# Weights read as float64 words: the clamp first, the sign out of a parametric rectifier, roundings and most shifts on ScalarE

## The chip, the cores and the metric

One Trainium2 chip, one of its cores. The metric is the device time of one execution in microseconds (us), the median of several runs. In the profile PE is the matrix engine (PEld its weight loads), DVE the vector engine, ACT the scalar engine, POOL GpSimd, and SP issues the DMAs.

## What is computed

Eight batches pass through windowed attention (eight heads, half of them with a plain window, half with a dilated one), and then through a mixing block with four weight matrices, `w_theta`, `w_tok_r`, `w_tok_i` and `w_ch`:

```python
scores = np.where(masks[None], scale * np.matmul(q, k.transpose(0, 1, 3, 2)), -1e9)
attn = softmax(scores);  x = np.matmul(attn, v)        # to (8, 576, 512)
theta = x @ w_theta
y = einsum('ts,bsd->btd', w_tok_r, x * cos(theta)) + einsum('ts,bsd->btd', w_tok_i, x * sin(theta))
u = x + y
out = u + np.maximum(u @ w_ch, 0.0)
```

The matrices `w_theta`, `w_tok_r`, `w_tok_i` and `w_ch` come as float64, so the kernel gets each word as two 32-bit halves and has to make a float32 of them itself.

## The kernel before, in words

PE multiplies pairs of rounded parts: each operand is a high part in a rounded format (`fp32r`) and a low part, the difference, and a product takes three matmuls (high times high, high times low, low times high). The high part is a cast (L351, L354 for weights), the low part a subtraction on POOL (L356).

There are 18 pieces of weight. `unpack` (L302 on) makes float32 of one, and `split` (L347 on) makes the two parts:

- `st_wth`, 4 pieces of 512 columns (`theta_unpack` and, later, `theta_split`), used by the matmuls `th`;
- `st_wtk`, the token weights, 5 pieces for each half g of the output (four of 576 columns, one of 288). The pieces of g = 0 become `wtkh`, `wtkl`; those of g = 1 become `late_wt_a`, `late_wt_b`. They are used by the matmuls `y`;
- `st_wch`, the channel weights, 4 pieces of 512 columns, which become `late_wc`, used by the matmuls `c`.

A piece of float64 words is loaded by DMA into a staging tile. C is the view of its high halves, T that of its low halves. Before, a piece passes through these steps: C times 2^-112 on ACT (L323); T shifted right by 29 (L326 on ACT for the odd pieces of wth and of the first token half, L329 on DVE for all others); C clamped on DVE (L331); C shifted left by 3 and joined with T by an OR on DVE (L333). This loses the sign. Even pieces get it back by a Sign on ACT (L337) and a product on POOL (L339), odd ones by an AND and OR on DVE (L342). Then the cast: on DVE for wth and the first token half (L351), on ACT for the rest (L354).

The staging tiles are borrowed. The five token pieces of g = 1 lie in `u3`, `xh1`, `xh2`, `xh3`, `xh0`, and `st_wch` 0 to 3 in `xh2`, `xh3`, `xh2`, `xh3`. So `st_wch1` is loaded after the fourth late token piece is split, `st_wch3` after `st_wch1` is split, and only after `st_wch3` does `xh3` become free for the parts of the attention result of batch 1 (`xh`, L549 to L555), which its `th` matmuls read. Of the trigonometric part the reader needs that `K` (the phase, L692 to L694), the sine and cosine (`g`, L700 and L651), the products with `xn` (L656, L706, L713) and the rounding of the products (`zh` L594, `zl` L599) run on ACT, DVE, ACT, DVE, DVE and POOL, one after another, in two pairs of buffers.

The order on each engine is fixed in the program. For batch 0 and the parts of batches 1 and 2 that run beside it, a planner (class `Order`) sets it: each task names the engine and a cost before each operation, and a list of ranks (`RANK`) breaks ties. From batch 1 on, `phase` writes the order out by hand. Changing which operations a weight needs therefore reorders the beginning of the program.

```python
EARLY = ("u0", "u1", "u2", "u3", "xh0")
LATE = ("u3", "xh1", "xh2", "xh3", "xh0")
LATE2 = ("xh2", "xh3", "xh2", "xh3")
```

Of the kernel before, what the change touches and what calls it, by code (L numbers as in the profile page):

```python
# [12 lines left out]
AF = mybir.ActivationFunctionType  # L13
ALU = mybir.AluOpType
# [3 lines left out]
DM = H * D  # L18
# [30 lines left out]

W_MAX = 2.0 ** -96 * (2.0 - 2.0 ** -3)


class Order:
# [13 lines left out]
    def pin(self, ins):  # L69
        if self.live:  # L70
            self.tc.keep_in_program_order(ins)

    def signal(self, event):
        self.events[event] = self.now
# [49 lines left out]
def dve(n):  # L124
    return 67 + 1.04 * n


def dve2(n):
    return 67 + 0.52 * n


def act(n):
    return 95 + 0.83 * n


def pool(n):
    return 2.36 * n


def dma(n):  # L140
    return 128 * 4 * n / 360.0
# [3 lines left out]
def build(ctx, tc, qT, kT, vw, wth, wtk, wch, masks, ident, outT):  # L145
    nc = tc.nc
# [13 lines left out]
    pin, go, signal = od.pin, od.go, od.signal  # L160
# [20 lines left out]
    def take(tag, bufs, n=None):  # L181
        n = reserve(tag) if n is None else n
        if od.live:
            if n >= bufs:
                yield None, ("free", tag, n - bufs)
            if n:
                yield None, ("got", tag, n - 1)
            signal(("got", tag, n))
        return n

    def give(tag, n):
        if od.live:
            signal(("free", tag, n))
# [57 lines left out]
    def late(tag, words):  # L251
        if tag not in late_w:
            late_w[tag] = hp.tile([128, words], F32R, tag=tag, name=f"late_{tag}")
        return late_w[tag]
# [47 lines left out]
    def unpack(src, sz, name, stage, early, n, key):  # L302

        tag = None
        if stage is None:
            st = hp.tile([128, 2 * DM], F32R, tag=f"wc{n}", name=f"st_{name}{n}")
        else:
            tag = stage
            yield from take(tag[0], 1, tag[1])
            st = hp.tile([128, 2, S], F32R, tag=tag[0], name=f"st_{name}{n}").rearrange("p a b -> p (a b)")  # L310
        raw = st[:, :2 * sz].bitcast(U32)
        yield "DMA", dma(2 * sz)
        if len(src.shape) == 3:
            pin(nc.sync.dma_start(raw.rearrange("p (c b) -> p c b", c=src.shape[1]), src.bitcast(U32)))
        else:
            pin(nc.sync.dma_start(raw, src.bitcast(U32)))
        signal(("raw", name, n))
        yield None, ("raw", name, n)
        pair = raw.rearrange("p (a b) -> p a b", b=2)
        Ci, Ti = pair[:, :, 1], pair[:, :, 0]  # L320
        C, T = Ci.bitcast(F32), Ti.bitcast(F32)
        yield "ACT", act(sz)
        pin(nc.scalar.activation(C, C, AF.Copy, scale=2.0 ** -112))  # L323
        if early and n % 2:
            yield "ACT", act(sz)
            pin(nc.scalar.activation(Ti, Ti, AF.Copy, scale=2.0 ** -29, bias=-0.5))  # L326
        else:
            yield "DVE", dve2(sz)
            pin(nc.vector.tensor_scalar(Ti, Ti, 29, None, op0=ALU.logical_shift_right))  # L329
        yield "DVE", dve2(sz)  # L330
        pin(nc.vector.tensor_scalar(C, C, W_MAX, -W_MAX, op0=ALU.min, op1=ALU.max))  # L331
        yield "DVE", dve(sz)
        pin(nc.vector.scalar_tensor_tensor(out=Ti, in0=Ci, scalar=3, in1=Ti,  # L333
                                           op0=ALU.logical_shift_left, op1=ALU.bitwise_or))
        if n % 2 == 0:
            yield "ACT", act(sz)
            pin(nc.scalar.activation(C, C, AF.Sign))  # L337
            yield "POOL", pool(sz)
            pin(nc.gpsimd.tensor_tensor(T, T, C, op=ALU.mult))  # L339
        else:  # L340
            yield "DVE", dve(sz)
            pin(nc.vector.scalar_tensor_tensor(out=Ti, in0=Ci, scalar=0x80000000, in1=Ti,  # L342
                                               op0=ALU.bitwise_and, op1=ALU.bitwise_or))
        signal(key)
        return T, tag

    def split(T, sz, dst, early, key):  # L347
        hi, lo = dst
        if early:
            yield "DVE", dve2(sz)  # L350
            pin(nc.vector.tensor_copy(hi, T))  # L351
        else:
            yield "ACT", act(sz)
            pin(nc.scalar.copy(hi, T))  # L354
        yield "POOL", pool(sz)
        pin(nc.gpsimd.tensor_tensor(lo, T, hi.bitcast(F32), op=ALU.subtract))  # L356
        signal(key)

    wth32, wths, wtks, wchs = {}, {}, {}, {}

    def theta_unpack(c):
        T, _ = yield from unpack(wth[:, c], DM, "wth", None, True, c, ("wth32", c))
        wth32[c] = T

    def theta_split(c):
        for st in range(5):
            yield None, ("th0", st, c)
        wths[c] = tuple(cp.tile([128, DM], F32R, name=f"wth{h}{c}") for h in "hl")
        yield from split(wth32[c], DM, wths[c], True, ("wth", c))
        signal(("wc", c))  # L370

    def token_weights(g, n, stage):
        cs = slice(HS * g, HS * g + HS)
        c = 2 * n
        src, sz = (wtk[:, c:c + 2, cs], 2 * HS) if n < 4 else (wtk[:, c, cs], HS)
        T, tag = yield from unpack(src, sz, f"wtk{g}_", stage, g == 0, n, None)
        if g:
            for p in range(NP):
                yield None, ("pv", 0, p)
            t, o = (late("wt_a", 8 * HS), 4 * HS * n) if n < 2 else (late("wt_b", 10 * HS), 4 * HS * (n - 2))  # L380
            dst = tuple(t[:, o + i * sz:o + i * sz + sz] for i in range(2))
        else:
            dst = tuple(cp.tile([128, sz], F32R, name=f"wtk{h}{n}") for h in "hl")
        wtks[g, n] = dst
        yield from split(T, sz, dst, g == 0, ("wtk", g, n))
        give(*tag)

    def chan_weights(c, stage):
        T, tag = yield from unpack(wch[:, c], DM, "wch", stage, False, c, None)
        yield None, ("wc", c)  # L390
        t = late(f"wc{c}", 2 * DM)
        wchs[c] = tuple(t[:, DM * i:DM * i + DM] for i in range(2))
        yield from split(T, DM, wchs[c], False, ("wch", c))
        give(*tag)

    def mask_of(pr, j):
# [460 lines left out]
    for n in range(5):  # L857
        go(token_weights(0, n, EA[n]), RANK["token_early"] + n * .01)
    go(second_loads(), RANK["load"])
    for c in range(NC):  # L860
        go(theta_split(c), RANK["theta_split"] + c * .01)
    for n in range(5):
        go(token_weights(1, n, LA[n]), RANK["token_late"] + n * .01)
    for n in range(NC):
        go(chan_weights(n, LA2[n]), RANK["chan"] + n * .01)
# [80 lines left out]
```

## Time and profile before

| | |
|---|---|
| median of 3 runs | 617.66 us (617.5 to 617.88) |
| profiled execution: own time | 619.21 us |
| profiled execution: span | 617.4 us |
| busy: PE, PEld | 571.2 us (93%), 516.0 us (84%) |
| busy: DVE, ACT, POOL | 390.5 us (63%), 350.3 us (57%), 234.6 us (38%) |
| mean granted PE clock | 0.975 |

The span is what the instructions of the one profiled execution take; its own time has the launch around it. A busy share is a mean over the whole span. The first fifth of this span looks different from the rest, so stretches of it have to be read by themselves. In rows of a timeline the columns are start, duration, engine, line, operation, tile written and read, and in brackets the idle time before it and what ended that. Where rows are grouped, there are sums and means instead.

### The profile page before, as it was taken

The page shows a single profiled execution, that of the slowest core. Times are in us where ns is not written, and L with a number is a line of the kernel's source. Part 1 is how long each engine was busy: PE and PEld are TensorE (multiplying, and loading weights), DVE is VectorE, ACT ScalarE, POOL GpSimd, SP SyncE. Part 2 cuts the span into 40 slices and gives each one's busy share as a digit, 9 for nine tenths or more (in the row PEclk, how much of TensorE's full clock was granted, in tenths as well). Part 3 has the DMA queues.
Part 4 walks back from the last instruction along what each step waited for, and adds up shares of the span by engine and source line. Part 5 has one row for each costly group of instructions (what it writes and reads, how often), then busy time and mean ns, then how long its engine had stood idle before and what let it go on. Part 6 is the DMA issues. An engine that isn't in the chain of part 4 may idle for free.

```text
span 617.4 us, 14052 instructions
## 1 busy us (share of the span) xinstructions
PE 571.2 (93%) x5428; PEld 516.0 (84%) x5428; DVE 390.5 (63%) x1290; ACT 350.3 (57%) x951; POOL 234.6 (38%) x218
## 2 busy tenths in 40 slices
PE   4796687869999999999999999999999999999997
PEld 3543576858999889988999889998999899999997
DVE  4899998995566557656576556666576565535112
ACT  1885637737753594647843685638844685457110
POOL 2347665452432252242523153243523162414320
PEclk9998797969999999999999999999999999999999
DMA  8971425700354006420354017420454013000102
GB/s 327 397 282 38 137 98 167 252 12 19 118 175 155 2 21 221 152 76 1 136 176 157 2 39 234 137 59 2 161 156 151 1 49 107 19 0 30 49 1 78
DMA packets 26722, 67.82 MB, mean 110 GB/s; under 512 B 2848, under 2 KB 3104, under 8 KB 26656
## 3 DMA queue, kind: packets, MB, share of 16 engines
q1 hardware_dynamic: 26656, 66.92, 31.8%
q8 instruction: 43, 0.70, 0.5%
q14 instruction: 23, 0.19, 0.1%
HBM read 57.48 MB, written 9.44 MB: 108 GB/s over the span
## 4 chain that ended last, share of the span: by engine, by line
PE 45%; DVE 27%; ACT 20%; issue 3%; POOL 2%; DMA 2%; SPq 0%; ACTq 0%; DVEq 0%; POOLq 0%
PE y L750 23%; PE c L779 9%; DVE pt L486 8%; ACT P L464 6%; PE th L636 4%; PE s L438 4%; PE o L573 3%; DVE P L413 3%; ACT zh L597 2%; ACT K L651 2%; DVE K L656 2%; ACT g L700 2%; ACT K L649 2%; POOL P L470 2%; DVE st_wtk L333 1%
## 5 line engine op out<-in xcount | busy, mean ns | idle before, releaser
L733 POOL TENSOR_TENSOR u<-x,u 128x288 fp32r<-128x288 f32 x64 | 55.0, 860 | 179.4 <-ACT u L731 160.0
L779 PE MATMUL c<-u,late_wc 128*128 128x288 f32 x768 | 114.6, 300 | 6.2 <-ACT late_wc L354 2.6
L486 DVE STREAM_TRANSPOSE pt<-P 32x288 f32<-32x288 f32 x224 | 105.1, 469 | 21.2 <-POOL P L470 18.1
L779 PEld LDWEIGHTS c<-u,late_wc 128*128 128x128 f32 x768 | 107.9, 190 | 11.4 <-ACT late_wc L354 3.1
L731 ACT CAST u<-x 128x288 fp32r<-128x288 f32 x64 | 27.4, 429 | 133.2 <-DVE x L728 133.2
L464 ACT ACTIVATE P<-P,mx 128x64 f32<-128x64 f32 x252 | 84.1, 336 | 19.6 <-DVE mx L458 19.6
L750 PE MATMUL y<-wtkh,zh 128*128 128x288 f32 x288 | 90.4, 314 | 1.6 <-DVE zh L594 1.4
L750 PE MATMUL y<-wtkh,zl 128*128 128x288 f32 x288 | 86.3, 300 | 1.0 <-POOL zl L599 1.0
L750 PE MATMUL y<-wtkl,zh 128*128 128x288 f32 x288 | 86.1, 299 | 0.1
L599 POOL TENSOR_TENSOR zl<-g,zh 128x512 fp32r<-128x512 f32 x40 | 52.6, 1314 | 79.5 <-ACT zh L597 69.7
L636 PE MATMUL th<-wthh,xh 128*128 128x512 f32 x224 | 75.9, 400 | 0.0
L750 PE MATMUL y<-late_wt_b,zh 128*128 128x288 f32 x320 | 69.5, 300 | 3.5 <-ACT late_wt_b L354 2.1
L728 DVE TENSOR_TENSOR x<-y,x 128x288 f32<-128x288 f32 x64 | 28.7, 450 | 65.5 <-PE y L750 62.7
L750 PE MATMUL y<-late_wt_a,zh 128*128 128x288 f32 x256 | 57.9, 308 | 2.5 <-DVE x L728 2.5
L750 PEld LDWEIGHTS y<-wtkh,zh 128*128 128x128 f32 x288 | 55.3, 192 | 4.5 <-DVE zh L594 2.1
L470 POOL TENSOR_TENSOR P<-P,sm 128x576 f32<-128x576 f32 x32 | 38.4, 1200 | 49.1 <-DVE sm L468 24.1
L750 PEld LDWEIGHTS y<-wtkh,zl 128*128 128x128 f32 x288 | 55.1, 191 | 1.5 <-POOL zl L599 1.5
L599 POOL TENSOR_TENSOR zl<-K,zh 128x512 fp32r<-128x512 f32 x32 | 41.5, 1296 | 38.9 <-ACT zh L597 35.9
L750 PEld LDWEIGHTS y<-wtkl,zh 128*128 128x128 f32 x288 | 55.2, 192 | 0.9 <-issue 0.5
L750 PEld LDWEIGHTS y<-late_wt_b,zh 128*128 128x128 f32 x320 | 52.0, 190 | 4.7 <-ACT late_wt_b L354 2.3
L413 DVE CUSTOM_DVE_ANT_0 P<-s,msk 128x64 f32<-128x64 f32 x288 | 45.4, 219 | 14.2 <-PE s L438 13.9
L636 PEld LDWEIGHTS th<-wthh,xh 128*128 128x128 f32 x224 | 42.1, 188 | 8.0
(107 smaller groups left out, 1138.5 us busy)
## 6 DMA issues: line engine op xcount, KB each, us to landing
q<-in_qT_dram SPq DMA_DIRECT2D x32, 576.0 KB, 4.3
va<-in_vw_dram SPq DMA_DIRECT2D x30, 320.0 KB, 3.1
out_dram<-x SPq DMA_DIRECT2D x32, 288.0 KB, 2.1
k<-in_kT_dram SPq DMA_DIRECT2D x28, 304.0 KB, 4.7
vb<-in_vw_dram SPq DMA_DIRECT2D x29, 256.0 KB, 3.2
st_wtk<-in_wtk_dram SPq DMA_DIRECT2D x8, 576.0 KB, 8.3
st_wth<-in_wth_dram SPq DMA_DIRECT2D x4, 512.0 KB, 8.6
st_wch<-in_wch_dram SPq DMA_DIRECT2D x4, 512.0 KB, 3.9
```

Source lines behind the costliest of these rows:

```text
L413: pin(nc.vector.tensor_tensor_reduce(out=P[:, n], in0=ps[:, n - g0], in1=msk[:, mask_of(pr, n)], op0=ALU.add, op1=ALU.max, scale=1.0, scal ...
L438: pe(nc.tensor.matmul(ps[64 * e:64 * e + 64, n - g0], q[:, qb], k[:, QB * qb:QB * qb + BW], start=True, stop=True))
L464: table(nc.scalar.activation(P[:, n], P[:, n], AF.Exp, bias=mx[:, n:n + 1], scale=SCALE, accum_out=sm[:, n:n + 1]))
L470: pin(nc.gpsimd.tensor_tensor(P, P, sm.unsqueeze(2).to_broadcast([128, NJ, BW]), op=ALU.mult))
L486: pin(nc.vector.transpose(pmats[b, pr][hh][k0:k0 + QB, :, QB * e:QB * e + QB], P[p0:p0 + QB, :, QB * o:QB * o + QB]))
L599: pin(nc.gpsimd.tensor_tensor(lo, z, hi.bitcast(F32), op=ALU.subtract))
L636: pe(nc.tensor.matmul(pt, l, r, start=(n == 0), stop=(n == 3 * NC - 1)))
L728: pin(nc.vector.tensor_tensor(x[:, ts], ps, x[:, ts], op=ALU.add))
L731: pin(nc.scalar.copy(uh[b, d][:, ts], x[:, ts]))
L733: pin(nc.gpsimd.tensor_tensor(ul[b, d][:, ts], x[:, ts], uh[b, d][:, ts].bitcast(F32), op=ALU.subtract))
L750: pe(nc.tensor.matmul(ps, l[:, cs], r, start=(n == 0), stop=(n == 3 * NK - 1)))
L779: pe(nc.tensor.matmul(ps, l[:, cs], r[:, ts], start=(n == 0), stop=(n == 3 * NC - 1)))
```

## The change

In `unpack` the clamp is made first, on the raw high halves (its bound is larger by 2^112, so it cuts the same values). The scaling pass on ACT becomes a parametric rectifier, `Prelu` with alpha = -2^32: a positive C is scaled by 2^-112, a negative one becomes positive and larger by 2^32. That is a bit of the exponent which the shift left by 3 moves to the place of the sign, so the sign needs no steps of its own. The low halves are shifted on ACT except for the even pieces of wth and of the first token half. In `split` the cast is always on ACT. Lines behind these functions stand 12 lower in number than before (L486 is L474).

```diff
-W_MAX = 2.0 ** -96 * (2.0 - 2.0 ** -3)
+W_MAX = 2.0 ** 16 * (2.0 - 2.0 ** -3)
...
+        yield "DVE", dve2(sz)
+        pin(nc.vector.tensor_scalar(C, C, W_MAX, -W_MAX, op0=ALU.min, op1=ALU.max))
         yield "ACT", act(sz)
-        pin(nc.scalar.activation(C, C, AF.Copy, scale=2.0 ** -112))
-        if early and n % 2:
+        pin(nc.scalar.activation(C, C, AF.Prelu, scale=2.0 ** -112, alpha=-2.0 ** 32))
+        if early and n % 2 == 0:
+            yield "DVE", dve2(sz)
+            pin(nc.vector.tensor_scalar(Ti, Ti, 29, None, op0=ALU.logical_shift_right))
+        else:
             yield "ACT", act(sz)
             pin(nc.scalar.activation(Ti, Ti, AF.Copy, scale=2.0 ** -29, bias=-0.5))
-        else:
-            yield "DVE", dve2(sz)
-            pin(nc.vector.tensor_scalar(Ti, Ti, 29, None, op0=ALU.logical_shift_right))
-        yield "DVE", dve2(sz)
-        pin(nc.vector.tensor_scalar(C, C, W_MAX, -W_MAX, op0=ALU.min, op1=ALU.max))
         yield "DVE", dve(sz)
         pin(nc.vector.scalar_tensor_tensor(out=Ti, in0=Ci, scalar=3, in1=Ti,
                                            op0=ALU.logical_shift_left, op1=ALU.bitwise_or))
-        if n % 2 == 0:
-            yield "ACT", act(sz)
-            pin(nc.scalar.activation(C, C, AF.Sign))
-            yield "POOL", pool(sz)
-            pin(nc.gpsimd.tensor_tensor(T, T, C, op=ALU.mult))
-        else:
-            yield "DVE", dve(sz)
-            pin(nc.vector.scalar_tensor_tensor(out=Ti, in0=Ci, scalar=0x80000000, in1=Ti,
-                                               op0=ALU.bitwise_and, op1=ALU.bitwise_or))
...
-    def split(T, sz, dst, early, key):
+    def split(T, sz, dst, key):
         hi, lo = dst
-        if early:
-            yield "DVE", dve2(sz)
-            pin(nc.vector.tensor_copy(hi, T))
-        else:
-            yield "ACT", act(sz)
-            pin(nc.scalar.copy(hi, T))
+        yield "ACT", act(sz)
+        pin(nc.scalar.copy(hi, T))
```

The rest of the diff drops the argument `early` where `split` is called.

The change also reorders the instructions. First DVE, where the first token weights are made. `st_wtk0_0` to `st_wtk0_3` are the staging tiles of g = 0, `wtkh0` and `wtkh1` their high parts. Before:

```order
L331 TENSOR_SCALAR st_wtk0_1_189<-st_wtk0_1_189 128x576
L329 TENSOR_SCALAR st_wtk0_2_223<-st_wtk0_2_223 128x576
L333 SCALAR_TENSOR_TENSOR st_wtk0_1_189<-st_wtk0_1_189 128x576
L331 TENSOR_SCALAR st_wtk0_2_223<-st_wtk0_2_223 128x576
L342 SCALAR_TENSOR_TENSOR st_wtk0_1_189<-st_wtk0_1_189 128x576
L351 CAST wtkh0_529<-st_wtk0_0_145 128x576
L351 CAST wtkh1_541<-st_wtk0_1_189 128x576
L333 SCALAR_TENSOR_TENSOR st_wtk0_2_223<-st_wtk0_2_223 128x576
```

DVE at the same place now:

```order
L324 TENSOR_SCALAR st_wtk0_1_189<-st_wtk0_1_189 128x576
L334 SCALAR_TENSOR_TENSOR st_wtk0_0_145<-st_wtk0_0_145 128x576
L324 TENSOR_SCALAR st_wtk0_2_223<-st_wtk0_2_223 128x576
L334 SCALAR_TENSOR_TENSOR st_wtk0_1_189<-st_wtk0_1_189 128x576
L324 TENSOR_SCALAR st_wtk0_3_277<-st_wtk0_3_277 128x576
L329 TENSOR_SCALAR st_wtk0_2_223<-st_wtk0_2_223 128x576
L324 TENSOR_SCALAR st_wtk0_4_302<-st_wtk0_4_302 128x288
L334 SCALAR_TENSOR_TENSOR st_wtk0_2_223<-st_wtk0_2_223 128x576
```

The sign step L342 and the two casts are gone from DVE's queue; the clamps (now L324) stand ahead of the steps on ACT that they used to follow.

Second, DVE around the last channel weight, `st_wch3`. `pt` are the transposed probabilities of batch 2, `x0_2` the residual of batch 0. Before:

```order
L486 STREAM_TRANSPOSE pt0_103<-P2_0_1177 32x9x32 x2
L329 TENSOR_SCALAR st_wch3_1360<-st_wch3_1360 128x512
L728 TENSOR_TENSOR x0_2_407<-y0_2_1_1382,x0_2_407 128x288
L331 TENSOR_SCALAR st_wch3_1360<-st_wch3_1360 128x512
L486 STREAM_TRANSPOSE pt1_105<-P2_0_1177 32x9x32 x2
L333 SCALAR_TENSOR_TENSOR st_wch3_1360<-st_wch3_1360 128x512
L486 STREAM_TRANSPOSE pt1_105<-P2_0_1177 32x9x32 x2
L342 SCALAR_TENSOR_TENSOR st_wch3_1360<-st_wch3_1360 128x512
```

DVE at the same place now:

```order
L474 STREAM_TRANSPOSE pt0_103<-P2_0_1178 32x9x32 x2
L334 SCALAR_TENSOR_TENSOR st_wch3_1271<-st_wch3_1271 128x512
L474 STREAM_TRANSPOSE pt0_103<-P2_0_1178 32x9x32 x2
L716 TENSOR_TENSOR x0_2_417<-y0_2_1_1295,x0_2_417 128x288
L474 STREAM_TRANSPOSE pt1_105<-P2_0_1178 32x9x32 x2
```

Before, eight transposes of this group (one more pair stands ahead of the rows shown) and the residual `x0_2` come ahead of DVE's last step on `st_wch3`; now two transposes do.

Third, PE where the last token product of batch 0, `y0_3`, ends. `th1_4` is the first theta product of batch 1, `c0_0` and `c0_1` the first two channel products. Before:

```order
L750 MATMUL y0_3_1_1438<-late_wt_b_1069,zl0_8_624 128x288
L779 MATMUL c0_0_0_1487<-u0_0_842,late_wc0_1270 128x288 x3
L779 MATMUL c0_0_0_1487<-u0_1_896,late_wc1_1314 128x288 x3
L779 MATMUL c0_0_0_1487<-u0_2_970,late_wc2_1456 128x288 x3
L779 MATMUL c0_0_0_1487<-u0_3_1129,late_wc3_1492 128x288 x3
L779 MATMUL c0_1_0_1514<-u0_0_842,late_wc0_1270 128x288 x3
L779 MATMUL c0_1_0_1514<-u0_1_896,late_wc1_1314 128x288 x3
L779 MATMUL c0_1_0_1514<-u0_2_970,late_wc2_1456 128x288 x3
L779 MATMUL c0_1_0_1514<-u0_3_1129,late_wc3_1492 128x288 x3
L641 MATMUL th1_4_1526<-wthh0_670,xh1_0_1205 128x512
```

PE at the same place now:

```order
L738 MATMUL y0_3_1_1416<-late_wt_b_869,zl0_7_759 128x288
L629 MATMUL th1_4_1449<-wthh0_640,xh1_0_1141 128x512
L631 MATMUL th1_4_1449<-wthl0_641,xh1_0_1141 64x512
L628 MATMUL th1_4_1449<-wthl1_661,xh1_1_1139 64x512
L629 MATMUL th1_4_1449<-wthh1_660,xh1_1_1139 128x512
L628 MATMUL th1_4_1449<-wthl2_669,xh1_2_1266 64x512
L629 MATMUL th1_4_1449<-wthh2_668,xh1_2_1266 128x512
L628 MATMUL th1_4_1449<-wthl3_686,xh1_3_1418 64x512
L629 MATMUL th1_4_1449<-wthh3_685,xh1_3_1418 128x512
L738 MATMUL y0_3_1_1416<-late_wt_b_869,zh0_8_609 128x288 x2
L738 MATMUL y0_3_1_1416<-late_wt_b_869,zl0_8_610 128x288
```

The 8 matmuls of `th1_4` have moved ahead of the last 3 of `y0_3` and of the 24 of `c0_0` and `c0_1`, which now come behind the rows shown.

More of the change, by code (lines that the diff above doesn't have):

```diff
@@ L368, in theta_split @@
         wths[c] = tuple(cp.tile([128, DM], F32R, name=f"wth{h}{c}") for h in "hl")
-        yield from split(wth32[c], DM, wths[c], True, ("wth", c))
+        yield from split(wth32[c], DM, wths[c], ("wth", c))
         signal(("wc", c))
@@ L384, in token_weights @@
         wtks[g, n] = dst
-        yield from split(T, sz, dst, g == 0, ("wtk", g, n))
+        yield from split(T, sz, dst, ("wtk", g, n))
         give(*tag)
@@ L392, in chan_weights @@
         wchs[c] = tuple(t[:, DM * i:DM * i + DM] for i in range(2))
-        yield from split(T, DM, wchs[c], False, ("wch", c))
+        yield from split(T, DM, wchs[c], ("wch", c))
         give(*tag)
```

## The prediction

> **What bounds the kernel now.** I read the span by stretches first: theta of batch 0 (20 to 42.6 us), its sine and cosine up to the first exponentials of batch 1 (to 72.1), the token products up to the second set of token weights (to 96.9), and the rest up to `th1_4`, the first theta product of batch 1 (136.9). Columns: stretch and length, then busy us (and instructions) of PE, PEld, DVE, ACT, POOL, then the granted PE clock, the DMA share and GB/s.
>
> ```profile
> 20.00:42.60 22.60, 19.20 (x196) 10.12 (x195) 20.40 (x50) 19.47 (x47) 8.23 (x7) 1.00 1.01 380
> 42.60:72.10 29.50, 19.61 (x124) 12.16 (x122) 29.39 (x60) 17.05 (x27) 20.65 (x16) 0.83 0.18 57
> 72.10:96.90 24.80, 21.24 (x237) 18.96 (x237) 24.34 (x94) 14.51 (x67) 16.27 (x13) 0.93 0.43 147
> 96.90:136.90 40.00, 29.46 (x274) 25.93 (x274) 36.63 (x103) 23.83 (x78) 22.18 (x21) 0.82 0.43 141
> 136.90:617.40 480.50, 472.08 (x4446) 440.33 (x4444) 269.22 (x909) 270.21 (x723) 161.87 (x153) 1.00 0.26 86
> ```
>
> From 136.9 us on PE is busy 472.08 of 480.5 us, 98%: PE is the bound, and the change does not touch that work. Ahead of it DVE is busy 110.76 of 116.9 us (95%), while PE stands idle for 27.4 of them and gets a lower clock. So the first part runs at DVE's pace, and if it becomes shorter, all the rest starts earlier by as much. What ends the first part is seen on the timelines of PE and POOL:
>
> ```profile
> 132.29 0.85 PE L779 MATMUL c<-u,late_wc 128*128 128x288 f32 x2 [2.55 <-ACT late_wc L354]
> 133.66 3.49 PE L779 MATMUL c<-u,late_wc 128*128 128x288 f32 x13 [0.52 <-POOL late_wc L356]
> 136.95 0.63 PE L641 MATMUL th<-wthh,xh 128*128 128x512 f32 x1
> 132.31 1.29 POOL L356 TENSOR_TENSOR late_wc<-st_wch,late_wc 128x512 fp32r<-128x512 f32 x1 [3.03 <-ACT late_wc L354]
> 134.67 1.27 POOL L555 TENSOR_TENSOR xh<-x,xh 128x512 fp32r<-128x512 f32 x1
> ```
>
> PE waits for the last channel weight, whose low part POOL finishes at 133.60. The staging tile `xh3` then goes to `xh1_3`, finished at 135.94, one microsecond before `th1_4`. These two events are the gate.
>
> **What leaves DVE.** 26 instructions: 8 sign steps (L342), all 9 casts (L351), and the 9 late shifts (L329; the five early even ones stay). Groups of 20 to 137 us, the last but one column is the mean in ns:
>
> ```profile
> L342 DVE SCALAR_TENSOR_TENSOR st_wtk<-st_wtk 128x576 uint32<-128x576 uint32 x4 | 4.8, 1194 | 0.0
> L342 DVE SCALAR_TENSOR_TENSOR st_wch<-st_wch 128x512 uint32<-128x512 uint32 x2 | 1.4, 688 | 0.0
> L342 DVE SCALAR_TENSOR_TENSOR st_wth<-st_wth 128x512 uint32<-128x512 uint32 x2 | 1.4, 677 | 0.0
> L351 DVE CAST wthh<-st_wth 128x512 fp32r<-128x512 f32 x4 | 4.5, 1137 | 0.0
> L351 DVE CAST wtkh<-st_wtk 128x576 fp32r<-128x576 f32 x4 | 2.1, 536 | 0.0
> L351 DVE CAST wtkh<-st_wtk 128x288 fp32r<-128x288 f32 x1 | 1.0, 991 | 0.0
> ```
>
> Busy time: 7.6 and 7.6 us. For the shifts, DVE's busy time on L329 by the same stretches:
>
> ```profile
> 20.00:42.60 22.60, 1.77 (x4) 1.00 1.01 380
> 42.60:72.10 29.50, 3.78 (x3) 0.83 0.18 57
> 72.10:96.90 24.80, 2.33 (x3) 0.93 0.43 147
> 96.90:136.90 40.00, 1.80 (x4) 0.82 0.43 141
> ```
>
> The five that stay are the four of the first stretch and one of 1.38 us (the 288-column piece), so 9.68 - 1.77 - 1.38 = 6.5 us go. Together 21.7 us. But these instructions are longer than their work. Minimum, median and maximum in ns:
>
> ```profile
> L342 DVE SCALAR_TENSOR_TENSOR st_wtk<-st_wtk x4: 700/1046/1985, 39.3 to 97.8; 128x576 uint32<-128x576 uint32 x4
> L351 DVE CAST wthh<-st_wth x4: 411/1310/1517, 57.0 to 65.2; 128x512 fp32r<-128x512 f32 x4
> L351 DVE CAST wtkh<-st_wtk x5: 447/452/991, 40.0 to 70.6; 128x576 fp32r<-128x576 f32 x4, 128x288 fp32r<-128x288 f32 x1
> L329 DVE TENSOR_SCALAR st_wch<-st_wch x4: 380/428/564, 106.1 to 125.6; 128x512 uint32<-128x512 uint32 x4
> L329 DVE TENSOR_SCALAR st_wtk<-st_wtk x8: 300/692/1574, 33.1 to 95.1; 128x576 uint32<-128x576 uint32 x6, 128x288 uint32<-128x288 uint32 x2
> ```
>
> The long ones lie under POOL instructions, as here:
>
> ```profile
> 56.95 1.29 POOL L599 TENSOR_TENSOR zl<-g,zh 128x512 fp32r<-128x512 f32 x1 [1.02 <-DVE zh L594]
> 57.01 1.52 DVE L351 CAST wthh<-st_wth 128x512 fp32r<-128x512 f32 x1
> ```
>
> The cast starts 0.06 us after POOL's subtraction and ends 0.29 after it. Three more rows of DVE's timeline, and POOL's time on the sign products (L339), summed over the four stretches:
>
> ```profile
> 25.47 0.69 DVE L333 SCALAR_TENSOR_TENSOR st_wth<-st_wth 128x512 uint32<-128x512 uint32 x1
> 26.08 0.17 DVE L467 TENSOR_SCALAR sm<-sm 128x9 f32<-128x9 f32 x1
> 27.99 1.09 DVE L331 TENSOR_SCALAR st_wth<-st_wth 128x512 f32<-128x512 f32 x1 [1.50 <-ACT st_wth L323]
> sum 116.90, POOL 11.62; mean POOL 2.90
> ```
>
> Unhindered, the 26 would take 8 x 0.69 + 4 x 0.41 + 4 x 0.45 + 0.30 + 4 x 0.45 + 0.30 + 4 x 0.43 = 13.1 us, and neighbours overlap by 0.08 us (the second of these rows starts at 26.08, the first ends at 26.16), so DVE's queue is relieved of 13.1 - 26 x 0.08 = 11.0 us of work: **-11.0**.
>
> The other 8.6 us are holds behind POOL. A hold goes away with the instruction, unless the next DVE instruction runs into the same POOL instruction. POOL loses the ten sign products (11.62 of its 67.3 us in these stretches, last row above), so there is also less to run into. Bounds: 0 and 8.6; lacking a row for what the neighbours do I take half, **-4.2**.
>
> The Trainium skill (SBUF — State Buffer, "Who interferes with whom") has a rule for this: of a DVE operation that uses two ports and a GpSimd operation, the one that starts first keeps the shared ports for its whole instruction and the other is blocked, while ACT waits for nobody. The trace agrees (1.52 us beside 0.41). By that rule a cast that moves to ACT is never held, which would favour the full 8.6 us; it does not say whether the next DVE instruction inherits the hold.
>
> **What else moves.** The clamp now needs only the DMA: DVE's idle time of 1.50 us before L331 (row above) falls away, **-1.5**. Two transposes, a residual, and 18 matmuls `c` on the chain of waits:
>
> ```profile
> 123.21 0.94 DVE L486 STREAM_TRANSPOSE pt<-P 32x288 f32<-32x288 f32 x2
> 126.11 0.45 DVE L728 TENSOR_TENSOR x<-y,x 128x288 f32<-128x288 f32 x1
> 160.74 2.40 PE c L779 x18
> ```
>
> In DVE's queue six transposes (0.47 us each) and one residual (0.45) no longer stand ahead of the last step on `st_wch3`: **-3.2**; that they come later costs nothing there, since `pt` of batch 2 is read after `th1`. On PE, 27 matmuls (24 `c`, 3 `y0_3`) now come behind `th1_4`. Before, they were done when the gate opened. At 2.40 us for 18 they take 3.6 us, after the gate: **+3.6**.
>
> **What ACT gets.** Nine casts and nine shifts, less ten signs. Rows of casts, shifts and scaling passes on ACT, and the time of the signs (L337):
>
> ```profile
> L354 ACT CAST late_wc<-st_wch 128x512 fp32r<-128x512 f32 x4 | 2.6, 656 | 5.0 <-DVE st_wch L342 4.7 <-POOL st_wch L339 0.2
> L326 ACT ACTIVATE st_wtk<-st_wtk 128x576 uint32<-128x576 uint32 x2 | 1.6, 806 | 0.0
> L326 ACT ACTIVATE st_wth<-st_wth 128x512 uint32<-128x512 uint32 x2 | 1.4, 694 | 0.0
> L323 ACT ACTIVATE st_wtk<-st_wtk 128x576 f32<-128x576 f32 x8 | 5.9, 739 | 0.0
> sum 116.90, ACT 6.67; mean ACT 1.67
> ```
>
> 9 x 0.67 + 4 x 0.81 + 4 x 0.69 + 0.5 - 6.67 = 5.9 us more. ACT is idle for 42.0 of the 116.9 us, so I cost them at 0. That cover is thin in the first stretch, where ACT is busy 19.47 of 22.6, but there only 3 signs go and two casts come. No row shows `Prelu`; the nearest is the scaling pass that it replaces, 0.74 us at 576 columns. I take the same time; a tenth more in 18 passes would be 1.3 us, also in idle time. The program has as many ACT table loads as before.
>
> **The sum.** -11.0 - 4.2 - 1.5 - 3.2 + 3.6 = -16.3. The profiled span is 617.4 and its execution 619.21; the median of the runs, 617.66, stands within 0.3 of the span, so I subtract from that: 601.4 us.
>
> **Rivals.**
>
> ACT becomes the bound (0.20). A weight now passes DVE, ACT, ACT, DVE, ACT, POOL, and ACT's queue also carries sines and exponentials in order; a cast that waits for DVE's combine holds the sine behind it. If the added 5.9 us lie on the path: -10.4, 607.3 us. For it: ACT at 86% in the first stretch. Against: 58 to 60% in the three others. The Trainium skill (ScalarE: Activation LUTs, "Rules for kernel authors") speaks for this rival: it gives multiplications and the like to VectorE. The trace agrees for one cast alone, 0.41 against 0.66 us.
>
> All holds go (0.25): the full 8.6 us, -20.7, 597.0 us. For it: POOL's ten products are gone. If PE's clock also recovers in the last stretch (it loses 29.46 x 0.18 = 5.3 us there), half of that leads to 594.3.
>
> Slower (0.05). PE runs in order, so `th1_4` now blocks 27 matmuls that were ready. If `xh1_3` is not finished earlier, the time is 617.66 + 3.6 = 621.3. It decides if `xh1_3` ends later than 135.94 - 3.6 = 132.3. For it: the tile `xh3` still passes through two weights and two DMAs in turn. Against: every one of them comes out of DVE's queue.
>
> No change (0.02): gate and 3.6 us balance.
>
> **How the numbers follow.** My forecast has 0.48: 601.4. Measurement tells changes above 0.2% (1.2 us) from none. All cases but the last two are faster: 0.93, same 0.02, slower 0.05. The range of 594 to 611 takes in both ends of the holds, ACT's 5.9 us and some waits more; outside it lie the slower rival, no change, and a tenth for steps that I have mis-sized.
>
> **What would show it.** DVE's busy time falls by 15 to 22 us, ACT's rises by about 6, POOL's falls by 11 to 12. The first exponentials of batch 1 start near 65 us (72.1 now), the last channel weight's low part ends near 114 to 117 (133.60), and `th1_4` follows `xh1_3` at once. PE after that is as before. I am wrong if DVE stays at 95% up to `th1_4` with remaining instructions that have become longer, if waits for `st_` tiles appear before DVE's combine (L334) and cost more than 6 us, or if `xh1_3` comes later than 132.3 us.

## The result, and the profile after

The changed kernel takes 601.4 us (median of 4 runs, 600.39 to 603.07) beside 617.77 us for the kernel before on the same chip: ratio 0.9729, 95% interval 0.9697 to 0.9762. The profiled execution has a span of 599.8 us (617.4 before). The forecast was 601.4; the total came out, most of its terms did not, and most of what follows is about that.

First the gate, on the timelines of POOL and PE of the changed kernel:

```profile
113.52 1.29 POOL L344 TENSOR_TENSOR late_wc<-st_wch,late_wc 128x512 fp32r<-128x512 f32 x1 [3.21 <-ACT late_wc L342]
116.33 1.27 POOL L543 TENSOR_TENSOR xh<-x,xh 128x512 fp32r<-128x512 f32 x1
112.46 0.39 PE L629 MATMUL th<-wthh,xh 128*128 128x512 f32 x1
115.57 0.45 PE L628 MATMUL th<-wthl,xh 128*64 128x512 f32 x1 [1.57 <-ACT xh L537]
117.51 3.09 PE L767 MATMUL c<-u,late_wc 128*128 128x288 f32 x12
122.00 1.85 PE L767 MATMUL c<-u,late_wc 128*128 128x288 f32 x12 [1.40 <-DVE x L716]
```

The last channel weight is ready at 114.81 (133.60 before) and `xh1_3` at 117.60 (135.94): the gate comes 18.3 us earlier. From it to the end of the span it is 482.2 us, before 481.5, so 0.7 us are given back behind the gate: -18.3 + 0.7 = -17.6, the difference of the spans of the two profiled executions.

Next the stretch from 20 us to this gate, one row of the windows for each kernel (columns as before: stretch and length, busy us of PE, PEld, DVE, ACT, POOL, PE clock, DMA, GB/s). Before:

```profile
20.00:135.94 115.94, 88.54 (x823) 66.20 (x822) 109.83 (x302) 74.86 (x216) 67.33 (x55) 0.88 0.48 169
```

The changed kernel, and behind it what follows its gate:

```profile
20.00:117.60 97.60, 83.93 (x819) 62.44 (x818) 85.70 (x269) 77.63 (x219) 53.37 (x43) 0.91 0.57 201
117.60:599.80 482.20, 472.34 (x4458) 441.96 (x4456) 271.68 (x917) 272.17 (x732) 163.72 (x156) 1.00 0.25 86
```

DVE's busy time fell by 24.1 us, its idle time (length less busy) rose from 6.1 to 11.9 us, and -24.1 + 5.8 is the -18.3 of the gate. The 24.1 can't be set beside the 21.7 of the removed instructions as they are, for two reasons: neighbours overlap, so that durations add up to more than busy time, and DVE does 33 instructions fewer in the stretch, not 26. The other seven now stand behind the gate (four transposes, a residual and two small steps of a softmax; the changed kernel):

```profile
118.76 0.17 DVE L455 TENSOR_SCALAR sm<-sm 128x9 f32<-128x9 f32 x1 [1.60 <-ACT P L452]
118.97 0.21 DVE L456 RECIPROCAL sm<-sm 128x9 f32<-128x9 f32 x1
120.51 0.95 DVE L474 STREAM_TRANSPOSE pt<-P 32x288 f32<-32x288 f32 x2 [1.33 <-POOL P L458]
121.49 0.46 DVE L716 TENSOR_TENSOR x<-y,x 128x288 f32<-128x288 f32 x1
122.57 0.95 DVE L474 STREAM_TRANSPOSE pt<-P 32x288 f32<-32x288 f32 x2
```

If the 26 are taken out of the trace of before, the time that its other instructions cover is 18.5 us shorter; without these seven as well it is 21.1 us shorter. So of the 24.1 us 18.5 are the removed instructions, 2.6 are work put off until behind the gate, and 3.0 are left for the instructions that stay and became shorter on balance.

Most of the 5.8 are new waits for ACT (7.8 us in all, before 2.9), 0.9 are for POOL. DVE's largest waits in this stretch of the changed kernel (engine, line, what it waited for: us in total, times, longest):

```profile
DVE sm L455 <- ACT P L452: 3.0, 3, 1.4
DVE pt L474 <- POOL P L458: 1.6, 2, 1.4
DVE st_wtk L334 <- ACT st_wtk L332: 1.5, 2, 1.3
DVE K L682 <- ACT K L680: 1.5, 3, 0.7
DVE g L701 <- ACT g L688: 1.2, 1, 1.2
```

Before, DVE's largest wait in its stretch was the 1.50 ahead of the clamp.

Then the holds behind POOL (a hold is the time by which an instruction is longer than its work). Minimum, median and maximum in ns of the combine of the channel weights (L333, now L334) and of the cast `zh` of `K`. Before:

```profile
L333 DVE SCALAR_TENSOR_TENSOR st_wch<-st_wch x4: 683/1310/1682, 108.9 to 128.4; 128x512 uint32<-128x512 uint32 x4
L594 DVE CAST zh<-K x4: 406/412/538, 51.1 to 71.6; 128x512 fp32r<-128x512 f32 x4
```

The same two groups in the changed kernel, and the rectifier:

```profile
L334 DVE SCALAR_TENSOR_TENSOR st_wch<-st_wch x4: 693/726/1127, 86.9 to 112.1; 128x512 uint32<-128x512 uint32 x4
L582 DVE CAST zh<-K x4: 414/1509/1656, 47.8 to 67.4; 128x512 fp32r<-128x512 f32 x4
L326 ACT ACTIVATE st_wtk<-st_wtk x10: 472/732/777, 33.2 to 75.3; 128x576 f32<-128x576 f32 x8, 128x288 f32<-128x288 f32 x2
```

Instructions that the change leaves alone lost holds (the combine, median 1.31 to 0.73 us), and others got some (the cast `zh`, 0.41 to 1.51). One of these casts with the POOL instruction above it:

```profile
47.60 1.62 POOL L344 TENSOR_TENSOR wtkl<-st_wtk,wtkh 128x576 fp32r<-128x576 f32 x1
47.85 1.66 DVE L582 CAST zh<-K 128x512 fp32r<-128x512 f32 x1
```

`Prelu` takes 0.73 us at 576 columns, as the Copy that it replaces did.

### The profile page after: what moved, and what is told of

Read it like the earlier page. It is cut to its first block, busy times and chain, and to the rows that moved or that the text cites. A ratio compares the mean times of both kernels' runs of the same rounds, so it can differ in the third digit from the quotient of the medians.

```text
span 599.8 us, 14024 instructions
## 1 busy us (share of the span) xinstructions
PE 567.4 (95%) x5428; PEld 513.8 (86%) x5428; DVE 367.2 (61%) x1264; ACT 354.5 (59%) x959; POOL 222.5 (37%) x208
## 4 chain that ended last, share of the span: by engine, by line
PE 42%; DVE 25%; ACT 21%; DMA 5%; issue 3%; POOL 3%; SPq 0%; ACTq 0%; POOLq 0%; DVEq 0%
PE y L738 21%; DVE pt L474 11%; PE c L767 9%; ACT P L452 7%; PE o L561 4%; PE th L624 3%; DVE P L401 3%; PE s L426 3%; ACT zh L585 2%; ACT K L639 2%; DVE K L644 2%; ACT g L688 2%; ACT K L637 2%; POOL P L458 2%; PE th L606 2%
## 5 line engine op out<-in xcount | busy, mean ns | idle before, releaser
L474 DVE STREAM_TRANSPOSE pt<-P 32x288 f32<-32x288 f32 x224 | 105.1, 469 | 23.5 <-POOL P L458 20.4
L767 PE MATMUL c<-u,late_wc 128*128 128x288 f32 x768 | 112.9, 299 | 2.2 <-DVE x L716 1.4
L452 ACT ACTIVATE P<-P,mx 128x64 f32<-128x64 f32 x252 | 84.1, 336 | 17.6 <-DVE mx L446 17.4
L738 PE MATMUL y<-late_wt_b,zh 128*128 128x288 f32 x320 | 68.0, 296 | 0.0
L458 POOL TENSOR_TENSOR P<-P,sm 128x576 f32<-128x576 f32 x32 | 38.2, 1197 | 43.6 <-DVE sm L456 22.2
```

The lines of the kernel that those rows point to most:

```text
L452: table(nc.scalar.activation(P[:, n], P[:, n], AF.Exp, bias=mx[:, n:n + 1], scale=SCALE, accum_out=sm[:, n:n + 1]))
L458: pin(nc.gpsimd.tensor_tensor(P, P, sm.unsqueeze(2).to_broadcast([128, NJ, BW]), op=ALU.mult))
L474: pin(nc.vector.transpose(pmats[b, pr][hh][k0:k0 + QB, :, QB * e:QB * e + QB], P[p0:p0 + QB, :, QB * o:QB * o + QB]))
L738: pe(nc.tensor.matmul(ps, l[:, cs], r, start=(n == 0), stop=(n == 3 * NK - 1)))
L767: pe(nc.tensor.matmul(ps, l[:, cs], r[:, ts], start=(n == 0), stop=(n == 3 * NC - 1)))
```

## The experiments

All ratios are to the kernel before on the same chip. For comparison they are also turned into us of 617.8: the change itself is -16.7 in that measure (interval 14.7 to 18.7). In the runs named "order held" every engine executes its instructions in the changed kernel's order, and only the edit differs; that is possible because the planner sees only the cost lines, which stay. The gate is the end of `xh1_3` on POOL in the profiled execution. Line numbers of some runs stand higher than those of the change, by up to 8 in the lines shown.

| run | median us | ratio (95% interval) | us against before | gate us |
|---|---|---|---|---|
| the change | 601.4 | 0.9729 (0.9697 to 0.9762) | -16.7 | 117.60 |
| casts on DVE again | 605.08 | 0.9771 (0.9735 to 0.9808) | -14.1 | 120.34 |
| late shifts on DVE again | 604.88 | 0.9775 (0.9729 to 0.9821) | -13.9 | 120.19 |
| sign steps again | 617.97 | 0.9979 (0.9961 to 0.9996) | -1.3 | 134.03 |
| all three again | 624.78 | 1.0088 (1.0057 to 1.0119) | +5.4 | 140.19 |
| sign steps, DVE's alone | 604.65 | 0.9767 (0.9745 to 0.9789) | -14.4 | 121.24 |
| sign steps, product off the chain | 613.2 | 0.9918 (0.9895 to 0.9941) | -5.1 | 129.19 |
| before, sign and clamp alone | 605.75 | 0.9793 (0.9765 to 0.9822) | -12.8 | 123.44 |
| before, casts and shifts alone | 611.03 | 0.9885 (0.9852 to 0.9918) | -7.1 | not read |
| the change in the order of before | 612.1 | 0.989 (0.985 to 0.9931) | -6.8 | 127.56 |
| `th1_4` behind `c` | 602.74 | 0.9747 (0.9717 to 0.9776) | -15.6 | 118.00 |
| shorter staging chain | 602.83 | 0.975 (0.9727 to 0.9773) | -15.4 | 116.39 |
| `zh` casts on ACT | 603.42 | 0.9769 (0.9743 to 0.9796) | -14.3 | 119.55 |

**One part put back at a time, order held.** The theory was that DVE's queue sets the pace and each instruction costs its unhindered time and half its holds; the rivals were ACT's pace, and the order.

The nine casts:

```diff
-        pin(nc.scalar.copy(hi, T))
+        if key[:1] == ("wth",) or key[:2] == ("wtk", 0):
+            pin(nc.vector.tensor_copy(hi, T))
+        else:
+            pin(nc.scalar.copy(hi, T))
```

> The changed kernel (601.4 us) with its nine early weight casts (wth, first token half) on DVE again, each at the place in the program where ACT makes it now, all else in the same order. Theory of the sum: 9 instructions of 0.41 to 0.45 us unhindered, less 0.08 us overlap each, are 3.0 us of DVE's queue, and half of their 3.9 us of holds 1.9 more: +4.9, 606.3 us, with bounds of +3.0 (no hold comes back) and +6.9 (all). Rival, ACT is the pace: ACT is relieved of 6.2 us, so the time stays or falls, 599 to 601.5. Rival, the order does it and not the instructions: within 1 us of 601.4.

The nine shifts:

```diff
-            pin(nc.scalar.activation(Ti, Ti, AF.Copy, scale=2.0 ** -29, bias=-0.5))
+            if early:
+                pin(nc.scalar.activation(Ti, Ti, AF.Copy, scale=2.0 ** -29, bias=-0.5))
+            else:
+                pin(nc.vector.tensor_scalar(Ti, Ti, 29, None, op0=ALU.logical_shift_right))
```

> The changed kernel with the nine shifts of the late weights (second token half, channel weights) on DVE again, each at the place where ACT makes it now. Theory of the sum: 3.8 us unhindered less 0.7 overlap is +3.1, with half of the 2.7 us of holds +4.5: 605.9 us (bounds 604.5 and 607.2). Rival, ACT is the pace: 599 to 601.5. Rival, these shifts lie in time that DVE has over since the change (it is busy 85.7 of the 97.6 us from 20 us to the gate): under +1.5, 603.

The sign steps (values unchanged; `ones` is a column of ones, so here, unlike in the kernel before, the product does not wait for the Sign):

```diff
+        if n % 2:
+            pin(nc.vector.scalar_tensor_tensor(out=Ti, in0=Ci, scalar=0, in1=Ti,
+                                               op0=ALU.bitwise_and, op1=ALU.bitwise_or))
+        else:
+            pin(nc.scalar.activation(C, C, AF.Sign))
+            pin(nc.gpsimd.tensor_tensor(T, T, ones.to_broadcast([128, sz]), op=ALU.mult))
```

> The changed kernel with the work of the sign steps added again, without effect on the values: for odd pieces a DVE step of the form of L342, for even pieces a Sign on ACT and a product with ones on POOL, each behind DVE's combine, all else in the same order. Theory of the sum: 8 DVE steps of 0.69 less 0.08 us are +4.9, half of their 2.1 us of holds +1.0: 607.3 us; what ten POOL products of 1.16 us do to DVE's other instructions comes on top, up to the 3 to 4 us that the change took from holds of instructions that it left in place, 611. Rival, the order does it: under +1.5, 603.

All three:

> The three edits at once (casts, late shifts, sign steps back), the order still that of the changed kernel and the clamp still first. Theory of the sum: -11.0 and -4.2 are given back, 616.6 us, with bounds of 612.4 and 620.8; what is left to the kernel before (617.77) is order and clamp, -1.1. Rival, the order does most of it: below 609. If the three singles add up to much more or less than this one, their costs are not additive, which neither counted on.

Casts and shifts cost 2.6 and 2.8 us by the ratios, a little below the lower bounds of 3.0 and 3.1. Their intervals overlap that of the change, so the ratios alone don't show these costs; the gate comes 2.7 and 2.6 us later in the two profiles. A cost speaks against ACT's pace alone, by which the time would have stayed or fallen. The sign steps cost 15.4, far above the 9.6 (611 us) that were the most I allowed. The singles add up to 20.8, all three together cost 22.2: additive within the intervals. And all three together are 5.4 us slower than the kernel before, which has the same operations but for the place of the clamp and the product's wait for the Sign: the order of the change, with the sign steps set right behind the combine, does not suit the operations of before.

**Which part of the sign steps costs.** The DVE steps of the odd pieces alone (the first branch above):

> Half of the edit that cost 16.6 us when the sign steps came back: only the DVE steps of the odd pieces stand behind the combine again, without effect on the values; no Sign on ACT, no product on POOL; order of the changed kernel. If the steps on the even pieces (ACT, then POOL, ahead of the cast) made the excess over the sum: 8 x 0.61 us and half of 2.1 us of holds, +6.0, 607.4 us. If DVE's steps themselves were underpriced: 612 to 618.

2.3 us where 6.0 were expected, so 13.1 of the 15.4 belong to the even pieces, whose Sign on ACT and product on POOL the sum had priced only by the holds that they cause. Then the product moved off the weight's way: it does the same work, but writes where nobody reads (this run leaves the Sign out):

```diff
-            pin(nc.scalar.activation(C, C, AF.Sign))
-            pin(nc.gpsimd.tensor_tensor(T, T, ones.to_broadcast([128, sz]), op=ALU.mult))
+            pin(nc.gpsimd.tensor_tensor(C, T, ones.to_broadcast([128, sz]), op=ALU.mult))
```

> As the run in which all sign steps came back (618.0 us), but POOL's product writes into the dead high halves instead of the weight, and ACT's Sign is left out: POOL does the same ten products at the same places, still behind DVE's combine, and no cast, no theta product of batch 0 and no staging tile's cast waits for them. The DVE steps alone cost 3.2 us, so 13.3 us belong to the even pieces. If these come from the weights' longer way (combine, product, cast, and DVE waiting later): about 605 to 608. If they come from POOL's time itself (holds of DVE behind POOL, POOL's other work queued behind a product that waits for its combine): 613 to 618.

9.3 of the 13.1 us stay, though no weight waits for a product any more: they come from POOL's time. The other 3.8 are the longer way and the Sign, not told apart. Holds of DVE are little of it: up to the gate DVE is busy 92.43 us with all sign steps and 90.81 with DVE's alone. What is left is POOL's queue, and one place shows how it acts. The run with all sign steps, around `zl8` and `zl0`, POOL and then ACT:

```profile
56.51 1.44 POOL L595 TENSOR_TENSOR zl<-g,zh 128x512 fp32r<-128x512 f32 x1
59.16 0.67 POOL L343 TENSOR_TENSOR st_wtk<-st_wtk,ones 128x288 f32<-128x288 f32 x1 [1.21 <-DVE st_wtk L336]
59.78 1.27 POOL L595 TENSOR_TENSOR zl<-K,zh 128x512 fp32r<-128x512 f32 x1
61.09 0.60 ACT L688 ACTIVATE K<-th 128x512 int32<-128x512 f32 x1 [6.18 <-POOL zl L595]
```

The same place with DVE's sign steps alone:

```profile
50.21 1.44 POOL L590 TENSOR_TENSOR zl<-g,zh 128x512 fp32r<-128x512 f32 x1
51.62 1.33 POOL L590 TENSOR_TENSOR zl<-K,zh 128x512 fp32r<-128x512 f32 x1
52.98 0.60 ACT L683 ACTIVATE K<-th 128x512 int32<-128x512 f32 x1 [4.37 <-POOL zl L590]
```

Here `zl0` follows `zl8` at once. With the products it stands behind one that waits 1.21 us for DVE's combine and takes 0.67, and ACT, which needs the buffer of `K`, waits for `zl0`: 6.18 us instead of 4.37. So a product on an engine that is busy 38% of the span (56% up to the gate of this run) delays the next phase, by its place in an in-order queue. The place makes 1.8 us: ACT's row is 8.1 us later than in the other run, and 6.3 of them were there before it (56.51 against 50.21 for `zl8`). In the run with the product off the chain the wait is 6.23 us, so this place makes 1.9 of the 8.0 us by which its gate is later (129.19 against 121.24). The other places were not followed one by one; that they act in the same way is argued, not shown. These runs put each product right behind its combine; in the kernel before the planner placed them.

**One part alone, planner free.** The planner sets a new order in both runs: the kernel before with the clamp first and the sign out of the rectifier, and the kernel before with casts and shifts moved alone:

```diff
-        pin(nc.scalar.activation(C, C, AF.Copy, scale=2.0 ** -112))
+        pin(nc.vector.tensor_scalar(C, C, W_MAX, -W_MAX, op0=ALU.min, op1=ALU.max))
+        pin(nc.scalar.activation(C, C, AF.Prelu, scale=2.0 ** -112, alpha=-2.0 ** 32))
...
-        pin(nc.vector.tensor_scalar(C, C, W_MAX, -W_MAX, op0=ALU.min, op1=ALU.max))
...
-        if n % 2 == 0:
...
```

> The kernel before (617.8 us) with the clamp first and the sign out of the rectifier alone; casts and late shifts stay on DVE, and the planner sets the order anew. By the sum of the prediction: 4.9 us of DVE's queue, 1.0 of their holds, 1.5 for the clamp, -7.4, 610.4 us; if POOL's ten products held other DVE instructions too, to 606. If the sign is worth 16.6 us in any order: 600 to 603, and then the casts and shifts add nearly nothing to it.

> The kernel before with the nine early casts and the shifts moved as in the change, but the sign steps and the clamp as before; the planner sets the order anew. By the sum: 3.0 + 3.1 us of queue and half of their 6.6 us of holds, -9.4, 608.4 us. By what these two cost when they were put back one by one (3.7 and 3.5 us): 610.6. If the chain of the sign steps sets the pace, and DVE's queue is only second to it: above 614.

Sign and clamp alone, with the planner's new order, give 12.8 of the 16.7 us. The windows of that kernel:

```profile
20.00:123.44 103.44, 84.70 (x818) 63.65 (x813) 99.30 (x285) 69.81 (x206) 54.14 (x44) 0.93 0.54 189
```

DVE is still busy 96% of the time, and its busy time is down by 10.5 us. Counted as above, 6.4 of them are the eight steps of L342, holds and all, 3.3 are nine other instructions that now stand behind the gate (four transposes again), and only 0.8 are left for the instructions that stay. Products of POOL did hold some of those; here is one from the trace of before, and the clamp on DVE that starts 0.47 us after it and ends 0.32 after it:

```profile
37.53 1.55 POOL L339 TENSOR_TENSOR st_wtk<-st_wtk 128x576 f32<-128x576 f32 x1 [2.45 <-ACT st_wtk L337]
38.00 1.40 DVE L331 TENSOR_SCALAR st_wtk<-st_wtk 128x576 f32<-128x576 f32 x1
```

But other instructions became longer in turn (the four casts `zh` of `K`, 0.44 to 0.97 us on the mean). Idle time falls by another 2.0, and the gate comes 12.5 us earlier: while DVE is the bound, what it is relieved of does not come back as idle time. Casts and shifts give 7.1 us alone, but only 4.0 on top of the sign steps (0.9793 against 0.9729). The profiled execution of the kernel with casts and shifts alone took 617.49 us, 6.5 above its median, so nothing is read from its trace.

**The order.** All operations of the change, each where the operation that it replaces stood in the kernel before; only the clamp, which now has to come first, stands right ahead of the rectifier:

> All operations of the changed kernel, clamp first included, but every engine in the order of the kernel before (each operation stands where the one it replaces stood, th1_4 behind c0_0 and c0_1). By the sum the two terms for the order cancel (-3.2 and +3.6), and this kernel has -11.0, -4.2 and -1.5: 601.1 us. If each order suits only the operations it was planned for, as the run of 624.8 us (operations of before in the order of the change, 7.0 above the kernel before) makes likely: 605 to 609.

Only -6.8 us, 10 short of the change and less than either case had expected. Its windows, and DVE's largest waits up to its gate:

```profile
20.00:127.56 107.56, 86.86 (x811) 64.97 (x806) 85.22 (x277) 78.20 (x223) 54.73 (x45) 0.90 0.52 182
```

```profile
DVE sm L458 <- ACT P L455: 4.0, 4, 1.3
DVE K L685 <- ACT K L683: 3.3, 1, 3.3
DVE x L719 <- PE y L741: 3.1, 2, 2.9
DVE K L647 <- ACT K L642: 2.6, 3, 1.1
```

DVE is busy 85.2 us, as little as in the change (85.7), but idle 22.3 us instead of 11.9. The same relief is worth 8.4 us at the gate in the old order and 18.3 in the new one. What DVE gives up becomes waits, mostly for ACT, unless the planner fills them. The clamp at its new place does not leave DVE idle: it waits 0.2 us in all for the DMA of a staging tile.

**The 27 matmuls behind `th1_4`.**

```diff
     def thetas(b):
+        for e in range(2):
+            yield None, ("ch", 0, e, 0)
         for st in STS:
```

> The changed kernel with th1_4 behind c0_0 and c0_1 again, as in the kernel before; the rest of the planner's order follows from that. The prediction charged 3.6 us for the 27 matmuls that now come behind it, so by it this kernel gains up to 3.6: 597.8 us. By the trace of the change, six of the eight matmuls of th1_4 ran before the gate while PE had nothing else, and c0_0 and c0_1 stood behind waits of their own (1.40 us on a residual): a gain of at most 2, 599.4 to 601.4. Rival: th1_4 later means its sine chain later, and the transposes xn behind it wait: 602 to 604.

No gain: 602.74 us, where the two cases with a gain had 597.8 and up to 601.4; the interval overlaps that of the change. PE of this run:

```profile
114.67 1.85 PE L767 MATMUL c<-u,late_wc 128*128 128x288 f32 x12 [1.27 <-DVE x L716]
118.11 2.51 PE L767 MATMUL c<-u,late_wc 128*128 128x288 f32 x15 [1.59 <-DVE x L716]
120.46 0.39 PE L629 MATMUL th<-wthh,xh 128*128 128x512 f32 x1
```

Half of the `c` matmuls wait for a residual on DVE until 118.11, behind the gate, so only the other half could run ahead of it. From the gate to the end it takes 483.5 us, with the change 482.2.

**The staging tile.**

```diff
-LATE2 = ("xh2", "xh3", "xh2", "xh3")
+LATE2 = ("xh1", "xh2", "xh1", "xh2")
```

> The changed kernel with the channel weights staged in xh1, xh2, xh1, xh2 instead of xh2, xh3, xh2, xh3, so that the chain of three pieces through xh3 (fourth late token piece, st_wch1, st_wch3) ahead of xh1_3 becomes one of one piece. If this chain set the gate at 117.60 us (10.7 us from the DMA of st_wch3 to its low part): the gate comes 3 to 9 us earlier and the time falls to 593 to 599. If DVE's and ACT's queues set it, and the chain only fits into them: 600 to 602.5. Slower, if xh1_1 and xh1_2, which now wait for the channel weights, delay th1_4 more than xh3 gains: 603 to 606.

```profile
102.96 1.32 POOL L344 TENSOR_TENSOR late_wc<-st_wch,late_wc 128x512 fp32r<-128x512 f32 x1 [1.31 <-ACT late_wc L342]
115.10 1.29 POOL L543 TENSOR_TENSOR xh<-x,xh 128x512 fp32r<-128x512 f32 x1
```

The last channel weight is ready at 104.28 instead of 114.81, and `xh1_3` still ends at 116.39, 1.2 us earlier, with no gain in time. In the changed kernel the weights' chain only fits into the queues; it does not set the gate.

**One step further.** The casts `zh` of batch 0 on ACT too, order held:

```diff
         if b == 0:
             yield "DVE", dve2(DM)
-            pin(nc.vector.tensor_copy(hi, z))
+            pin(nc.scalar.copy(hi, z))
```

> The changed kernel with one more step in its own direction: the nine casts zh of batch 0 (L582) go from DVE to ACT, each at its place, the order held. They take DVE 8.4 us from 20 us to the gate (five of 0.42 us, four near 1.5, held behind POOL) and would take ACT about 9 x 0.66 = 5.9. If DVE still sets the pace: 595 to 599 us. If what DVE gives up now goes into waits for ACT (DVE's idle time rose from 6.1 to 11.9 us with the change): 600 to 603. If ACT has become the bound (80% busy up to the gate): 604 to 608. The cast stands between DVE's product and POOL's subtraction, in the chain that the next phase waits for on ACT.

```profile
20.00:119.55 99.55, 82.76 (x812) 61.76 (x812) 78.80 (x259) 81.68 (x226) 52.54 (x43) 0.93 0.56 197
```

DVE is relieved of 6.9 us more, and the gate comes 1.95 us later: its idle time is now 20.8 us. 603.42 us is just above the middle case, by which what DVE gives up goes into waits; moving these casts to ACT gains nothing in this order. By the Trainium skill (ScalarE: Activation LUTs, "Rules for kernel authors") `relu`, `max`, `min`, additions and multiplications belong on VectorE; it names neither casts nor shifts. Taken for such simple steps, the rule fits this last run, and it does not fit the casts and shifts of the change, which gained 4.0 us on ACT, with the order that the planner made for them.

## Why the prediction was right, and where it was not

DVE's queue did set the pace, so the way and the rough size were right; that the total of -16.3 us came out so closely was luck, since errors of several us cancelled. The terms, and what the two profiled executions (spans 617.4 and 599.8) show for each:

| term | forecast, us | shown, us |
|---|---|---|
| the 26 instructions that leave DVE, with holds | -11.0 - 4.2 | -18.5 |
| work of DVE that now stands behind the gate | -3.2 | -2.6 |
| instructions of DVE that stay | 0 | -3.0 |
| DVE's idle time up to the gate (clamp, ACT) | -1.5 + 0 | +5.8 |
| PE behind the gate | +3.6 | +0.7 |
| sum | -16.3 | -17.6 |

- **The bound.** Right: with DVE at 95% of the stretch, the kernel with the sign steps gone gained at the gate what DVE lost, and idle time did not grow. PE behind the gate stayed as it was, 0.7 us longer.
- **Queue relief and half of the holds, -11.0 - 4.2.** Too small by 3.3, and 3.0 more came from instructions that stay. So holds went as the rival "all holds go" had it, and somewhat beyond. The step that failed is the half, taken for lack of a row (half of 8.6 is 4.3, too; the sum took 4.2). A hold can pass on to another instruction, as I had reckoned: the four casts `zh` of `K` are 3.3 us longer (1.8 to 5.1 us in all). More was lost than passed on. How much of that is due to POOL's ten products is not settled: with the order held they lengthen DVE's busy time by 1.6 us (90.81 to 92.43), and with the sign steps gone and the order new only 0.8 us went from what stays. By the Trainium skill (SBUF — State Buffer, "Who interferes with whom") the blocked one of the two waits for the other's whole instruction; the pair of product and clamp above agrees, with the clamp ending 0.32 us after the product.
- **ACT at 0.** This is the error the other way. DVE's idle time rose by 5.8 us, 4.9 of it in waits for ACT, though ACT had 20% of the stretch idle after the change. Free time on an engine is no cover when the work is a step in a chain, or stands in the queue ahead of one: DVE's combine waited 1.5 us for shifts on ACT (`st_wtk`, L334 for L332), and DVE waited longer than before for exponentials and phases that ACT also makes (3.0 us on `sm`, 1.5 on `K`). ACT as a bound was a rival at 0.20, and it took part of the gain, while DVE's relief gave more than forecast.
- **The sign steps.** Priced at 4.9 and about 1 us of holds, with 1.5 for the clamp: -7.4, measured -12.8. At the gate it was 6.4 for the steps and 2.0 of idle time, 8.4 together; the rest is mainly the 3.3 of work that the new order put behind the gate. The product's place in POOL's queue, ahead of the subtractions `zl`, was not in the sum at all; the runs with the order held show that ten products cost there (9.3 us, where products stand right behind their combine). How much of the 12.8 this makes in the kernel before's own order is not measured.
- **Casts and shifts.** 3.0 + 3.1 of queue and 3.3 of holds, -9.4 together; measured -4.0 on top of the sign steps, and -7.1 alone.
- **Clamp first, -1.5.** DVE's wait of 1.50 for ACT before the clamp is gone from the list of waits. It was not run alone.
- **Six transposes and a residual, -3.2, and 27 matmuls, +3.6.** Two terms for the order with a sum of +0.4. The first was near: 2.6 us of DVE's work went behind the gate, four transposes, the residual and two small steps. But the order as a whole was worth about -10: the change in the order of before has only -6.8. The prediction looked at two places of the order and left out that the planner fills DVE's waits everywhere. The +3.6 is 0.7 by the time behind the gate, and putting `th1_4` back gained nothing.
- **What would show it.** The first exponentials of batch 1 start at 65.75 (forecast near 65), the last low part ends at 114.81 (114 to 117), POOL's busy time falls by 12.1 (11 to 12), and waits for `st_` tiles before L334 are under 2 us. DVE's fell by 23.3 over the whole span (15 to 22), ACT's rose by 4.2 (about 6). `th1_4` did not follow `xh1_3` at once: six of its eight matmuls ran ahead of it, from 112.46.

## What to carry to other kernels

Where an in-order engine is 95% busy, count what leaves it with its holds, and count apart what the new order only puts off until later; then look for the engine that it waits for next, since idle share there is no cover for steps in a chain. A small instruction on an idle engine is not free if it waits in a queue ahead of something that another phase needs. Where a planner sets the order, an edit of operations and the order that goes with it are one change: here the old order was 10 us worse with the new operations, and the new order, with the sign steps put in by hand, 5 us worse with the old ones.

## What the runs showed of the hardware

- A parametric rectifier with a slope of -2^32 runs in the time of a scaling Copy: 0.73 us (median, mostly 576 columns), where the Copy took 0.74 on the mean at 576.
- A hold behind POOL fell on other DVE instructions when the queues came in another order: the unchanged cast `zh` of `K` went from a median of 0.41 us to 1.51, and the unchanged combine of the channel weights from 1.31 to 0.73.
- A product of 0.67 us on POOL, an engine busy for 38% of the span, delayed the next phase on ACT by 1.8 us (6.18 against 4.37 us of waiting), because it stood in POOL's queue ahead of a subtraction and waited there for DVE.
